# Attention over a cache with a gated FFN, one decode step: rounds of two heads on halves of the partitions, for single heads on all of them

## The chip, the cores and the metric

The kernel runs on one core of a Trainium2 chip. A core has TensorE (PE in the profile; PEld is its weight load), VectorE (DVE), ScalarE (ACT), GpSimd (POOL) and SyncE (SP), which here only issues transfers; sixteen DMA engines carry what SP and ACT issue. The metric is the device time of one execution in microseconds (us), the median of several runs; lower is better. A profile is one further execution, taken by the hardware profiler; its span is a little shorter than its time.

## The reference

```python
# B = 2, D = 448, H = 16 heads, Sk = 4096, Dh = 256, F = 1792, all float32
q = (x @ wq).reshape(B, 1, H, Dh).transpose(0, 2, 1, 3)
scores = einsum("bhqd,bhkd->bhqk", q, k_cache) * Dh ** -0.5
p = softmax(scores)
a = einsum("bhqk,bhkd->bhqd", p, v_cache).transpose(0, 2, 1, 3).reshape(B, 1, H * Dh) @ wo
h = maximum(x @ w1 + b1, 0) ** 2
b = h @ w2 + b2
g = sigmoid((x * gate_w).sum(-1))
out = g * a + (1 - g) * b
```

K and V are 2 x 16 x 4096 x 256 float32, 134 MB each; wq and wo are 7.3 MB each, w1 and w2 3.2 MB each. There is one query per batch row, so every byte of K and V is used once.

## The kernel before

The kernel goes through 32 pairs (batch b, head h), `pairs`, with b changing fastest. For a pair the 4096 keys lie as 32 consecutive keys on each of 128 partitions: one load of 4 MB (`load_kv`, line 131), a row of 32 KB for each partition, contiguous in memory. VectorE multiplies K by q in place (`times_q`, line 289, in pieces of 4, 12 and 16 keys, `LEAD` and `LEAD2`) and sums the rows (`row_sums`, line 296) into 32 scores a partition. `maximum` (line 302) takes the largest over a partition on VectorE and over the partitions with a matmul against the identity; `softmax` (line 309) has ScalarE write the exponentials into `pw`, a tensor in which every pair has its own two columns. `values` (line 335) multiplies V by these weights in 16 matmuls (two records each in the profile), four of which stand side by side in the array, and collects in one of two PSUM tiles, `po_bufs`. A unit is a group of heads that collect in one tile: four heads each, and at the end three and one. When a unit is done, `norm` works out the normalising factors, `take` copies the tile out, `turn` transposes it and normalises it, and `project` multiplies it by that unit's part of wo (8 matmuls) into `acc`. The last unit's part of wo and most of w2 go instead through `late` into `fin` at the very end.

All of K, V, wq, w1, w2 and wo come through one ring of five slots of 32 KB a partition (`ring`). A load into a slot can be issued only when everything has been read that the slot held before. Almost all loads are issued by SP in the order of the code, so an issue that waits for its slot holds back all issues behind it; loads already issued go on. In pair i the code issues K of pair i+1, then V of pair i, and then wq, w1, w2 or wo where one is due (w1 at i = 2, 0.46 MB of w2 at i = 4, wo of a unit at its last pair). The code is in the engines' order (`manual_schedule`): nothing reorders it. VectorE works one pair ahead of PE: in pair i it takes the maximum of pair i, then multiplies and sums K of pair i+1.

wq (448 x 4096) comes in three loads of 256, 128 and 64 input rows; the last 64 rows are laid on 128 partitions in two halves. `project_q` does 32 matmuls, four for each load and column block, and `make_q` spreads q of two heads at a time over the partitions.

Of the kernel before, what the change touches and what calls it, by code (L numbers as in the profile page):

```python
# [8 lines left out]
F32 = mybir.dt.float32  # L9
# [7 lines left out]
def kernel(  # L17
# [14 lines left out]
    nc = tc.nc  # L32
# [5 lines left out]
    CF = D // P  # L38
    R0 = CF * P
    RR = D - R0  # L40
    assert 2 * RR == P and B == 2 and CF == 3
    NK = S // P
    J = 32
    NCH = NK // J
# [7 lines left out]
    QH = QB // DH  # L52
    DQ = D // 4
    RING = 5
    WH = 2
    W2_CUTS = (4, 8, 11)
    LEAD = 4
# [4 lines left out]
    ring = ctx.enter_context(tc.tile_pool(name="ring", bufs=RING))  # L62
# [8 lines left out]


    wq_t = []

    def load_wq():

        ta = slot("wqa")
        nc.sync.dma_start(ta, wq[:2 * P, :].rearrange("(p c) n -> p (c n)", c=2))
        tb_ = slot("wqb")
        nc.sync.dma_start(tb_[:, :N], wq[2 * P:R0, :])  # L80
        nc.sync.dma_start(tb_[:, N:N + N // 2], wq[R0:, :].rearrange("r (s n) -> (r s) n", s=2))  # L81
        wq_t.extend([ta[:, :N], ta[:, N:], tb_[:, :N], tb_[:, N:N + N // 2]])

    w1_t = []

    def load_w1():
        t = slot("w1")
        nc.sync.dma_start(t[:, :2 * F], w1[:2 * P, :].rearrange("(p c) n -> p (c n)", c=2))
        nc.sync.dma_start(t[:, 2 * F:3 * F], w1[2 * P:R0, :])
        nc.sync.dma_start(t[:, 3 * F:3 * F + F // 2], w1[R0:, :].rearrange("r (s n) -> (r s) n", s=2))  # L90
        w1_t.extend([t[:, :F], t[:, F:2 * F], t[:, 2 * F:3 * F], t[:, 3 * F:3 * F + F // 2]])
# [39 lines left out]
    def load_kv(src, i, nm, cuts=(), between=None):  # L131
        b, h = pairs[i]
        v = src[b, h].rearrange("(n p j) d -> n p j d", p=P, j=J)
        tiles = []
        for n in range(NCH):
            t = slot(f"{nm}{b}_{h}_{n}").rearrange("p (j d) -> p j d", d=DH)
            at = [0, *(cuts if n == NCH - 1 else ()), J]
            for lo, hi in zip(at, at[1:]):
                nc.sync.dma_start(t[:, lo:hi, :], v[n, :, lo:hi, :])
                if between is not None and hi < J:  # L140
                    between()
            tiles.append(t)
        return tiles

    pairs = [(b, h) for h in range(H) for b in range(B)]
    last = len(pairs) - 1


    load_wq()
# [25 lines left out]
    for k in range(HG):  # L175
        for b in range(B):
            pw[k, b] = const.tile([P, NK // 2, 4 * HG], F32, name=f"pw{k}_{b}")
            nc.vector.memset(pw[k, b], 0.0)

# [6 lines left out]
    xr2 = const.tile([B, RR, 2], F32, name="xr2")  # L186
    nc.vector.tensor_copy(xr2, x2[:, R0:].unsqueeze(2).to_broadcast([B, RR, 2]))
    pxt = ps.tile([P, 512], F32, name="pxt", tag="sm")
    pxv = pxt[:, :(CF + 1) * B].rearrange("p (c b) -> p c b", b=B)
    for c in range(CF + 1):  # L190
        src = (x2[:, c:2 * P:2] if c < 2 else x2[:, c * P:(c + 1) * P] if c < CF
               else xr2.rearrange("b r s -> b (r s)"))
        nc.tensor.matmul(pxv[:, c, :], src, ident[:B, :B], start=True, stop=True)
    xT = const.tile([P, CF + 2, B], F32, name="xT")
    nc.vector.tensor_copy(xT[:, :CF, :], pxv[:, :CF, :])
    for s in range(2):
        nc.vector.tensor_scalar(xT[:, CF + s, :], pxv[:, CF, :], eo[:, s:s + 1], None, op0=ALU.mult)
# [19 lines left out]
    qs = const.tile([P, NQ // 4, QB], F32, name="qs")  # L217

    def project_q():
        for c in range(CF + 1):  # L220
            for n in range(NQ):
                a, gq = divmod(n, 4)
                if c < CF:
                    lt, rhs = xT[:, c, :], wq_t[c][:, n * QB:(n + 1) * QB]
                else:
                    half, m = divmod(n, NQ // 2)
                    lt, rhs = xT[:, CF + half, :], wq_t[c][:, m * QB:(m + 1) * QB]
                nc.tensor.matmul(po_bufs[a][32 * gq:32 * gq + B, :], lt, rhs, start=(c == 0), stop=(c == CF))  # L228
        for a in range(NQ // 4):
            nc.scalar.activation(qs[:, a, :], po_bufs[a], AF.Copy, scale=scale)  # L230
# [3 lines left out]
    def make_q(b, n):  # L234

        a, gq = divmod(n, 4)
        r = 32 * gq + b
        pq = ps.tile([P, 512], F32, name=f"pq{b}_{n}", tag="pq")
        nc.tensor.matmul(pq, ident[:, r:r + 1].to_broadcast([P, P]), qs[:, a, :], start=True, stop=True)  # L239
        t = work.tile([P, QB], F32, name=f"q{b}_{n}", tag=f"q{b}")  # L240
        nc.scalar.activation(t, pq, AF.Copy)  # L241
        for k in range(QH):
            q_sb[b, n * QH + k] = t[:, k * DH:(k + 1) * DH]
# [6 lines left out]
    h_sb = shared[:B, :F]  # L250

    def ffn_hidden():
        ph = ps.tile([P, 512], F32, name="ph", tag="pq")
        for c in range(CF + 1):
            for n in range(FB):
                if c < CF:
                    lt, rhs = xT[:, c, :], w1_t[c][:, n * D:(n + 1) * D]
                else:
                    half, m = divmod(n, FB // 2)
                    lt, rhs = xT[:, CF + half, :], w1_t[c][:, m * D:(m + 1) * D]  # L260
                nc.tensor.matmul(ph[32 * n:32 * n + B, :D], lt, rhs, start=(c == 0), stop=(c == CF))
        for n in range(FB):
            nc.scalar.activation(h_sb[:, n * D:(n + 1) * D], ph[32 * n:32 * n + B, :D], AF.Copy)

    def ffn_turn():
        hv = h_sb.rearrange("b (p c) -> b c p", c=FC)
        pt = ps.tile([P, FC, B], F32, name="pt", tag="sm")
        for c in range(FC):
            nc.tensor.matmul(pt[:, c, :], hv[:, c, :], ident[:B, :B], start=True, stop=True)  # L269
        return pt  # L270

    def ffn_square(pt):
        hb = const.tile([P, FC, B], F32, name="hb")
        nc.vector.tensor_tensor(hb, pt, b1T.unsqueeze(2).to_broadcast([P, FC, B]), op=ALU.add)
# [5 lines left out]
    kts, s_t, rs_t, rl_t, oT = {}, {}, {}, {}, {}  # L280

    def parts(lo, hi):

        while lo < hi:
            e = min(hi, (lo // J + 1) * J)
            yield lo // J, lo % J, lo % J + e - lo
            lo = e

    def times_q(i, lo, hi):

        b, h = pairs[i]
        for n, a, e in parts(lo, hi):
            kt = kts[i][n][:, a:e, :]
            nc.vector.tensor_tensor(kt, kt, q_sb[b, h].unsqueeze(1).to_broadcast([P, e - a, DH]), op=ALU.mult)  # L294

    def row_sums(i, lo, hi):
        if lo == 0:
            s_t[i] = work.tile([P, NK], F32, name=f"s{i}", tag="s")
        for n, a, e in parts(lo, hi):
            nc.vector.tensor_reduce(s_t[i][:, n * J + a:n * J + e], kts[i][n][:, a:e, :], axis=AX.X, op=ALU.add)  # L300

    def maximum(i):
# [3 lines left out]
        nc.tensor.matmul(mt[:, :P], m.to_broadcast([P, P]), ident, start=True, stop=True)  # L306
        return mt

    def softmax(i, mt):
        b, h = pairs[i]  # L310
        nb = work.tile([P, 1], F32, name=f"nb{i}", tag="nb")
        nc.vector.tensor_reduce(nb, mt[:, :P], axis=AX.X, op=ALU.max, negate=True)  # L312
        u, k = unit_of[h]
        c = B * k + b
        if c == 0:
            rs_t[u] = work.tile([P, B * len(units[u])], F32, name=f"rs{u}", tag="rs")
        nc.scalar.activation(pw[k, b][:, :, 2 * c:2 * c + 2], s_t[i].rearrange("p (m s) -> p m s", s=2), AF.Exp,  # L317
                             bias=nb, accum_out=rs_t[u][:, c:c + 1])

    def sums(u):  # L320
        sm = ps.tile([P, 512], F32, name=f"sum{u}", tag="sm")
        nc.tensor.matmul(sm[:, :B * len(units[u])], ones_pp, rs_t[u], start=True, stop=True)  # L322
# [12 lines left out]
    def values(i, vt, lo=0, hi=NK // 2):  # L335
        b, h = pairs[i]
        u, k = unit_of[h]
        n = len(units[u])
        po = po_bufs[u % 2]
        for m in range(lo, hi):  # L340
            r = 32 * (m % 4)
            j = 2 * m
            nc.tensor.matmul(po[r:r + 4 * n, :], pw[k, b][:, m, :4 * n],  # L343
                             vt[j // J][:, j % J:j % J + 2, :].rearrange("p j d -> p (j d)"),
                             start=(k == 0 and b == 0 and m < 4), stop=(k == n - 1 and b == B - 1 and m >= NK // 2 - 4))
# [56 lines left out]
    kts[0] = load_kv(k_cache, 0, "k")  # L402
    project_q()
    make_q(0, 0)
    make_q(1, 0)
    for n in range(NCH):
        times_q(0, n * J, (n + 1) * J)
# [123 lines left out]
```

## Time and profile before

| | us |
|---|---|
| median of 3 runs (lowest to highest) | 683.41 (683.37 to 683.63) |
| the profiled execution | 683.23 |
| its span | 681.4 |
| PE busy | 296.5 (44%) |
| VectorE busy | 581.1 (85%) |
| ScalarE busy | 37.9 (6%) |

An engine that is busy for a large share of the span need not be what the time hangs on. In this profile three things are to be read together: the row of the DMA engines' busy share, the rate in GB/s in a stretch that is clear of the start and the end, and what SP waited for before it issued. The two stretches in which the transfers are not at full rate, the first and the last slice, are the start and the end of the program.

### The profile page before, as it was taken

To read this page: it belongs to the slowest core of one execution; us is meant where nothing else is said; L and a number is where in the kernel's file an instruction comes from. 1 tells how busy PE (TensorE), PEld (TensorE's weight loads), DVE (VectorE), ACT (ScalarE), POOL (GpSimd) and SP (SyncE) were. 2 spreads that over 40 slices of the span, in tenths; PEclk is the share of its full clock that TensorE was granted. 3 is DMA by queue.
4 is the path that set the end of the run, shared out by engine and by line. 5 is a ranking of instruction groups with operands and counts; after the bars stand their busy time and mean duration, and the time that the engine had idled before them with its cause. 6 is when DMAs were issued, how large, how long until landed. Compare 5 with 4: busy or idle time off the path is not lost.

```text
span 681.4 us, 3865 instructions
## 1 busy us (share of the span) xinstructions
PE 296.5 (44%) x1598; PEld 96.8 (14%) x1598; DVE 581.1 (85%) x233; ACT 37.9 (6%) x113; POOL 0.7 (0%) x6
## 2 busy tenths in 40 slices
PE   4413445543359134433347543422455712443066
PEld 1000111400115001000014110000112200101013
DVE  3299997989896999999996999899997899999990
ACT  0200001000010000000001000000001000000000
POOL 0000000000000000000000000000000000000000
PEclk9856667787656776665667865567667757667579
DMA  8999999999999999999999999999999999999996
GB/s 370 435 433 435 430 425 431 426 434 436 431 437 430 431 431 431 430 431 431 432 426 441 431 431 432 433 429 431 431 430 423 432 431 431 430 435 437 423 419 270
DMA packets 12380, 289.79 MB, mean 425 GB/s; under 512 B 1478, under 2 KB 1612, under 8 KB 2892
## 3 DMA queue, kind: packets, MB, share of 16 engines
q1 hardware_dynamic: 12200, 289.55, 99.1%
q8 instruction: 12, 0.20, 0.1%
q10 hardware_dynamic: 164, 0.02, 0.0%
q14 instruction: 4, 0.03, 0.0%
HBM read 289.56 MB, written 0.00 MB: 425 GB/s over the span
## 4 chain that ended last, share of the span: by engine, by line
DMA 59%; DVE 37%; PE 2%; issue 0%; SPq 0%; ACT 0%; DVEq 0%; ACTq 0%
DMA k<-in_A_k_cache_dram 56%; DVE k L294 18%; DVE s L300 18%; DMA w<-in_B_w_dram 3%; PE acc L385 1%; PE po_buf L343 1%; DVE nb L312 0%; PE mt L306 0%; DVE m L304 0%; PE fin L390 0%; SPq L111 0%; ACT oT L378 0%; SPq L81 0%; ACT pw L317 0%; SPq L80 0%
## 5 line engine op out<-in xcount | busy, mean ns | idle before, releaser
L294 DVE TENSOR_TENSOR k<-k,q 128x3072 f32<-128x3072 f32 (+3 forms) x94 | 285.1, 3057 | 75.7 <-DMA k<-in_A_k_cache_dram 75.7
L300 DVE TENSOR_REDUCE s<-k 128x32 f32<-128x8192 f32 x32 | 278.0, 8686 | 2.2
L343 PE MATMUL po_buf<-v,pw 128*16 128x512 f32 (+2 forms) x1024 | 181.1, 857 | 218.3 <-DMA v<-in_A_v_cache_dram 217.4
L343 PEld LDWEIGHTS po_buf<-v,pw 128*16 128x16 f32 (+2 forms) x1024 | 36.7, 123 | 349.8 <-issue 319.7
L306 PE MATMUL mt<-ident,m 128*128 128x128 f32 x64 | 19.1, 389 | 136.2 <-DVE m L304 136.2
L317 ACT ACTIVATE pw<-s,nb 128x32 f32<-128x32 f32 x32 | 10.3, 323 | 544.0 <-DVE nb L312 544.0
L306 PEld LDWEIGHTS mt<-ident,m 128*128 128x128 f32 x64 | 11.9, 233 | 167.7 <-DVE m L304 117.1
L385 PE MATMUL acc<-wo,oT 128*2 128x448 f32 x48 | 22.9, 640 | 4.9 <-ACT oT L378 4.9
L239 PE MATMUL pq<-qs,ident 128*128 128x512 f32 x32 | 24.6, 868 | 0.0
L372 PEld LDWEIGHTS ot<-rl,shared 128*128 128x128 f32 x96 | 18.8, 304 | 0.0
L372 PE MATMUL ot<-rl,shared 128*128 128x8 f32 x96 | 18.8, 338 | 0.0
L312 DVE TENSOR_REDUCE nb<-mt 128x1 f32<-128x128 f32 x32 | 9.1, 284 | 1.7 <-PE mt L306 1.7
L241 ACT ACTIVATE q<-pq 128x512 f32<-128x512 f32 x16 | 9.4, 588 | 9.5 <-PE pq L239 9.5
L322 PE MATMUL sum<-rs,ones_pp 128*128 128x8 f32 (+2 forms) x10 | 2.8, 349 | 11.3 <-ACT pw L317 11.3
L354 ACT ACTIVATE shared<-po_buf 128x1024 f32<-128x1024 f32 x6 | 5.8, 1020 | 30.9 <-PE po_buf L343 30.9
L385 PEld LDWEIGHTS acc<-wo,oT 128*2 128x2 f32 x48 | 4.3, 94 | 21.3 <-issue 16.2
L239 PEld LDWEIGHTS pq<-qs,ident 128*128 128x128 f32 x32 | 6.9, 262 | 1.3 <-ACT qs L230 0.9
L269 PE MATMUL pt<-ident,shared 2*128 2x2 f32 x28 | 7.0, 378 | 0.0
L269 PEld LDWEIGHTS pt<-ident,shared 2*128 2x128 f32 x28 | 6.9, 336 | 0.1
L304 DVE TENSOR_REDUCE m<-s 128x1 f32<-128x32 f32 x32 | 5.9, 186 | 1.1
L317 ACT ACTIVATION_READ_ACCUMULATOR pw<-s,nb 128x1 f32 x32 | 6.0, 187 | 0.0
L228 PE MATMUL po_buf<-wqa,xT 128*2 128x512 f32 x32 | 5.6, 858 | 0.8 <-DMA wqa<-in_A_wq_dram 0.8
(62 smaller groups left out, 55.3 us busy)
## 6 DMA issues: line engine op xcount, KB each, us to landing
k<-in_A_k_cache_dram SPq DMA_DIRECT2D x32, 4096.0 KB, 40.0
v<-in_A_v_cache_dram SPq DMA_DIRECT2D x30, 4096.0 KB, 31.6
wo<-in_A_wo_dram SPq DMA_DIRECT2D x4, 1792.0 KB, 34.1
v<-in_A_v_cache_dram SPq DMA_DIRECT2D x3, 2048.0 KB, 25.9
wqa<-in_A_wq_dram SPq DMA_DIRECT2D x1, 4096.0 KB, 12.4
w<-in_B_w_dram SPq DMA_DIRECT2D x3, 896.0 KB
wqb<-in_A_wq_dram SPq DMA_DIRECT2D x1, 2048.0 KB, 16.9
v<-in_A_v_cache_dram SPq DMA_DIRECT2D x2, 1024.0 KB, 24.5
```

What stands on the lines that cost most here:

```text
L239: nc.tensor.matmul(pq, ident[:, r:r + 1].to_broadcast([P, P]), qs[:, a, :], start=True, stop=True)
L241: nc.scalar.activation(t, pq, AF.Copy)
L269: nc.tensor.matmul(pt[:, c, :], hv[:, c, :], ident[:B, :B], start=True, stop=True)
L294: nc.vector.tensor_tensor(kt, kt, q_sb[b, h].unsqueeze(1).to_broadcast([P, e - a, DH]), op=ALU.mult)
L300: nc.vector.tensor_reduce(s_t[i][:, n * J + a:n * J + e], kts[i][n][:, a:e, :], axis=AX.X, op=ALU.add)
L304: nc.vector.tensor_reduce(m, s_t[i], axis=AX.X, op=ALU.max)
L306: nc.tensor.matmul(mt[:, :P], m.to_broadcast([P, P]), ident, start=True, stop=True)
L312: nc.vector.tensor_reduce(nb, mt[:, :P], axis=AX.X, op=ALU.max, negate=True)
L317: nc.scalar.activation(pw[k, b][:, :, 2 * c:2 * c + 2], s_t[i].rearrange("p (m s) -> p m s", s=2), AF.Exp, bias=nb, accum_out=rs_t[u][:, c ...
L343: nc.tensor.matmul(po[r:r + 4 * n, :], pw[k, b][:, m, :4 * n], vt[j // J][:, j % J:j % J + 2, :].rearrange("p j d -> p (j d)"), start=(k = ...
L372: nc.tensor.matmul(ptv[:, j, :], ov[:, s, j, :], rl_t[u][:, :, s], start=(s == 0), stop=(s == 1))
L385: nc.tensor.matmul(acc[:, :D], oT[g][:, j, :], wo_sb[g][:, j, :], start=False, stop=(g == NG - 2 and j == HJ - 1))
```

## The change

A round is now two heads of one batch row: head 2n on partitions 0 to 63 and head 2n+1 on partitions 64 to 127, each partition with 64 consecutive keys. There are 16 rounds. K of a round is loaded in two halves of 32 keys a partition (`load_k`, line 138 of the changed kernel), each 4 MB in rows of 32 KB that lie 64 KB apart in memory; V in two such loads as well, but into one tile (`load_v`). The five slots become a ring of three slots of 32 KB, for K, w1, w2 and wo, and one slot of 64 KB (`wide`), for wq and then V. SP's order in round i is V of round i, then w1, w2 or wo where due (w1 at round 1, w2 at round 3, wo of a unit at the unit's last round), then the second half of K of round i+1 and the first half of K of round i+2. `units` ends with two units of two heads. A unit is taken, turned and projected in the round in which it ends, not in the next. wq and w1 come in one load each: seven half rows of the input matrix stand on a partition, and `times_x` adds them up in seven steps with four rows of x instead of two, 28 and 14 matmuls.

```diff
-    RING = 5
+    V_CUTS = (32, 48, 56)
-    ring = ctx.enter_context(tc.tile_pool(name="ring", bufs=RING))
+    ring = ctx.enter_context(tc.tile_pool(name="ring", bufs=3))
+    wide = ctx.enter_context(tc.tile_pool(name="wide", bufs=1))
...
+    def wide_slot(name):
+        return wide.tile([P, NK * DH], F32, name=name, tag="wide")
...
     def load_wq():
+        t = wide_slot("wq")[:, :D * N // P]
+        nc.sync.dma_start(t, wq.rearrange("(r k) (s n) -> (r k s) n", k=XR, s=2).rearrange(
+            "(p k) n -> p (k n)", k=XR))
+        return t
...
+    rounds = [(b, n) for n in range(H // 2) for b in range(B)]
+    last = len(rounds) - 1
+
+    def of_round(src, i):
+        b, n = rounds[i]
+        return src[b, 2 * n:2 * n + 2].rearrange("h (p j) d -> (h p) j d", p=PH)
+    def load_k(i, half):
+        t = slot(f"k{i}_{half}").rearrange("p (j d) -> p j d", d=DH)
+        nc.sync.dma_start(t, of_round(k_cache, i)[:, half * J:(half + 1) * J, :])
+        kts[i, half] = t
+    def load_v(i, cuts=(J,)):
+        t = wide_slot(f"v{i}").rearrange("p (j d) -> p j d", d=DH)
+        at = [0, *cuts, NK]
+        for lo, hi in zip(at, at[1:]):
+            nc.sync.dma_start(t[:, lo:hi, :], of_round(v_cache, i)[:, lo:hi, :])
+        return t
...
-    units = [list(range(g * HG, (g + 1) * HG)) for g in range(NG - 1)] + [list(range(H - HG, H - 1)), [H - 1]]
+    units = [list(range(g * HG, (g + 1) * HG)) for g in range(NG - 1)] + [[H - 4, H - 3], [H - 2, H - 1]]
...
+    def times_x(out, t, width, n):
+        for a in range(XR):
+            c, half = divmod(a, 2)
+            for g in range(n):
+                nc.tensor.matmul(out[32 * g:32 * g + 2 * B, :width], xT[:, half, c].rearrange("p s b -> p (s b)"),
+                                 t[:, (a * n + g) * width:(a * n + g + 1) * width],
+                                 start=(a == 0), stop=(a == XR - 1))
...
+        for e in range(2):
+            at = slice(e * PH, (e + 1) * PH)
+            c = B * (k + e) + b
+            nc.scalar.activation(pw[k, b][at, :, 2 * c:2 * c + 2], s_t[i][at].rearrange("p (m s) -> p m s", s=2), AF.Exp,
+                                 bias=nb[at], accum_out=rs_t[u % 2][at, c:c + 1])
...
+    load_k(0, 0)
+    load_k(0, 1)
+    load_k(1, 0)
     project_q()
+    make_q(0)
+    make_q(1)
...
+    for i, (b, n) in enumerate(rounds):
+        u, k = unit_of[2 * n]
+        done = b == B - 1 and k == len(units[u]) - 2
+        vt = load_v(i, V_CUTS) if i == last else load_v(i)
+        if i == 1:
+            w1_t = load_w1()
+        if i == 3:
+            load_w2_early()
+        if done and u < NG - 1:
+            load_wo(u)
         if i == last - 1:
+            load_wo(NG - 1)
         if i == last:
             load_w2_late()
         if i < last - 1:
+            load_k(i + 1, 1)
+            load_k(i + 2, 0)
+        if i == last - 2:
+            load_k(last, 1)
+        mt = maximum(i)
         if i < last:
+            times_q(i + 1, 0, 0, LEAD)
         softmax(i, mt)
...
+        values(i, vt)
+        if done:
+            take(u)
+            turn(u)
+            if u < NG - 1:
+                project(u)
...
+        rest(i + 1)
...
+    values(last, vt, p2, p3)
     late_wo(H - 3)
+    values(last, vt, p3, NK // 2)
     take(NG)
-    late_wo(H - 2)
     turn(NG)
     late_w2(0, W2_CUTS[0])
+    late_wo(H - 2)
     late_wo(H - 1)
```

SP's queue where the first unit (heads 0 to 3) ends, before. A name has the batch row and the head (`v1_3` is V of batch row 1, head 3), `wo0` is the unit's part of wo.

```order
L139 DMA v0_3_0_447<-in_A_v_cache_dram 128x8192
L139 DMA k0_4_0_481<-in_A_k_cache_dram 128x8192
L139 DMA v1_3_0_483<-in_A_v_cache_dram 128x8192
L125 DMA wo0_485<-in_A_wo_dram 128x3584
L139 DMA k1_4_0_528<-in_A_k_cache_dram 128x8192
L139 DMA v0_4_0_530<-in_A_v_cache_dram 128x8192
```

The same place now. A name has the round, and K its half (`k4_1` is the second half of K of round 4).

```order
L102 DMA w2_0_420<-in_B_w2_dram 128x896
L122 DMA wo0_422<-in_A_wo_dram 128x3584
L141 DMA k4_1_424<-in_A_k_cache_dram 128x8192
L141 DMA k5_0_426<-in_A_k_cache_dram 128x8192
L148 DMA v4_522<-in_A_v_cache_dram 128x8192 x2
L141 DMA k5_1_525<-in_A_k_cache_dram 128x8192
```

The small part of w2 now stands next to wo, both in the ring of three, behind V of round 3 and ahead of both halves of K.

PE's queue at the end of the first unit, before: values of the last two heads, with maxima (`mt`) and the sums between, turn (L372) and projection (L385).

```order
L343 MATMUL po_buf0_92<-v0_3_0_447,pw3_0_111 16x512 x16
L306 MATMUL mt7_489<-ident_85,m7_487 128x128
L322 MATMUL sum0_496<-rs0_206,ones_pp_90 128x8
L239 MATMUL pq1_2_503<-qs_145,ident_85 128x512
L343 MATMUL po_buf0_92<-v1_3_0_483,pw3_1_113 16x512 x16
L306 MATMUL mt8_534<-ident_85,m8_532 128x128
L372 MATMUL ot0_542<-rl0_501,shared_147 128x8 x16
L385 MATMUL acc_96<-wo0_485,oT0_559 2x448 x8
```

And now:

```order
L308 MATMUL mt3_430<-ident_85,m3_428 64x64 x2
L325 MATMUL sum0_439<-rs0_107,ones_pp_90 128x8
L345 MATMUL po_buf0_92<-v3_417,pw2_1_105 16x512 x32
L373 MATMUL ot0_480<-rl0_444,shared_145 128x8 x16
L386 MATMUL acc_96<-wo0_422,oT0_497 2x448 x8
L464 MATMUL acc_96<-w2_0_420,hT_144 2x448 x2
```

The values of a round are 32 matmuls in a row, and turn and projection follow them with no maximum between.

SP's queue at the end of the program, before:

```order
L139 DMA k0_15_0_1361<-in_A_k_cache_dram 128x8192
L139 DMA k1_15_0_1363<-in_A_k_cache_dram 128x8192
L139 DMA v1_14_0_1365<-in_A_v_cache_dram 128x8192
L139 DMA v0_15_0_1408<-in_A_v_cache_dram 128x4096
L128 DMA wo3_1410<-in_A_wo_dram 128x4x896
L139 DMA v0_15_0_1408<-in_A_v_cache_dram 128x4096
L139 DMA v1_15_0_1449<-in_A_v_cache_dram 128x4096
L139 DMA v1_15_0_1449<-in_A_v_cache_dram 128x2048 x2
```

And now:

```order
L141 DMA k15_1_1157<-in_A_k_cache_dram 128x8192
L148 DMA v14_1228<-in_A_v_cache_dram 128x8192 x2
L125 DMA wo3_1231<-in_A_wo_dram 128x4x896
L148 DMA v15_1281<-in_A_v_cache_dram 128x8192
L148 DMA v15_1281<-in_A_v_cache_dram 128x4096
L148 DMA v15_1281<-in_A_v_cache_dram 128x2048 x2
```

Of the last loads only wo stands between V of the last two rounds, which share a slot.

More of the change, by code (lines that the diff above doesn't have):

```diff
@@ L37 @@
     N = H * DH
[L38 to L44, printed above, removed]
+    XR = 7
+    XC = (XR + 1) // 2
+    assert D * 2 == P * XR and B == 2
+    PH = P // 2
+    NK = S // PH
+    J = NK // 2
     HG = 4
@@ L129, in load_wo @@
             wo_sb[g] = tv.rearrange("p (h j n) -> p h j n", h=HG, j=NJ)
[L131 to L149, printed above, removed]
+    rounds = [(b, n) for n in range(H // 2) for b in range(B)]
[3 more added lines that the diff above has]
+        return src[b, 2 * n:2 * n + 2].rearrange("h (p j) d -> (h p) j d", p=PH)
+    kts = {}
+    def load_k(i, half):
[7 more added lines that the diff above has]
+            nc.sync.dma_start(t[:, lo:hi, :], of_round(v_cache, i)[:, lo:hi, :])
+        return t
+    wq_t = load_wq()
     x2 = const.tile([B, D], F32, name="x2")
@@ L178 @@
             nc.vector.memset(pw[k, b], 0.0)
+    rs_t = []
+    for n in range(2):
+        rs = const.tile([P, B * HG], F32, name=f"rs{n}")
+        nc.vector.memset(rs, 0.0)
+        rs_t.append(rs)
     eo = const.tile([P, 2], F32, name="eo")
@@ L214 @@
     nc.tensor.matmul(acc[:, :D], gd[:, 1, :], b2r, start=True, stop=False)
-    qs = const.tile([P, NQ // 4, QB], F32, name="qs")
+    qs = const.tile([P, QB], F32, name="qs")
     def project_q():
[L220 to L230, printed above, removed]
@@ L232 @@
-    q_sb = {}
[L234 to L243, printed above, removed]
+        times_x(po_bufs[0], wq_t, QB, NQ // 2)
@@ new lines, in project_q, with make_q @@
+        nc.scalar.activation(qs, po_bufs[0], AF.Copy, scale=scale)
+    q_sb = {}
+    def make_q(i):
+        b, n = rounds[i]
+        a, g = divmod(n, NQ // 2)
+        r = 32 * g + B * a + b
+        pq = ps.tile([P, 512], F32, name=f"pq{i}", tag="pq")
+        for k in range(2):
+            nc.tensor.matmul(pq[k * PH:(k + 1) * PH, :DH], ident[:, r:r + 1].to_broadcast([P, PH]),
+                             qs[:, k * DH:(k + 1) * DH], start=True, stop=True)
+        q_sb[i] = work.tile([P, DH], F32, name=f"q{i}", tag=f"q{b}")
+        nc.scalar.activation(q_sb[i], pq[:, :DH], AF.Copy)
@@ L246, with ffn_hidden @@
     hT = const.tile([P, FC, B], F32, name="hT")
     shared = const.tile([P, 2 * HG * DH], F32, name="shared")
-    h_sb = shared[:B, :F]
-    def ffn_hidden():
+    h_sb = shared[:2 * B, :F]
+    def ffn_hidden(w1_t):
         ph = ps.tile([P, 512], F32, name="ph", tag="pq")
[L254 to L263, printed above, removed]
+        times_x(ph, w1_t, D, FB // 2)
+        hv = h_sb.rearrange("r (a g n) -> r g a n", a=2, n=D)
+        for g in range(FB // 2):
+            nc.scalar.activation(hv[:, g], ph[32 * g:32 * g + 2 * B, :D].unsqueeze(1).to_broadcast([2 * B, 2, D]), AF.Copy)
@@ L273, in ffn_square @@
         hb = const.tile([P, FC, B], F32, name="hb")
-        nc.vector.tensor_tensor(hb, pt, b1T.unsqueeze(2).to_broadcast([P, FC, B]), op=ALU.add)
+        for a in range(2):
+            at = slice(a * PH, (a + 1) * PH)
+            nc.vector.tensor_tensor(hb[at], pt[at, :, a * B:(a + 1) * B], b1T[at].unsqueeze(2).to_broadcast([PH, FC, B]),
+                                    op=ALU.add)
         nc.vector.tensor_scalar(hb, hb, 0.0, None, op0=ALU.max)
@@ L335, in values @@
     def values(i, vt, lo=0, hi=NK // 2):
-        b, h = pairs[i]
-        u, k = unit_of[h]
+        b, h = rounds[i]
+        u, k = unit_of[2 * h]
         n = len(units[u])
@@ L341, in values @@
             r = 32 * (m % 4)
[L342 to L345, printed above, removed]
+            nc.tensor.matmul(po[r:r + 4 * n, :], pw[k, b][:, m, :4 * n], vt[:, 2 * m:2 * m + 2, :].rearrange("p j d -> p (j d)"),
+                             start=(k == 0 and b == 0 and m < 4), stop=(k == n - 2 and b == B - 1 and m >= NK // 2 - 4))
     o_sb = {}
@@ L444 @@
         if done:
             norm(u, sums(u))
-        if h % QH == QH - 1 and h + 1 < H:
-            make_q(b, (h + 1) // QH)
-        if k == 0 and b == 0 and u > 0:
-            turn(u - 1)
-            if u < NG:
-                project(u - 1)
+        if i == last:
+            break
+        values(i, vt)
[4 more added lines that the diff above has]
+                project(u)
+        if i == 1:
+            ffn_hidden(w1_t)
+        if i == 2:
+            pt = ffn_turn()
@@ L471 @@
-        if i < last - 1:
-            values(i, vt)
-            if done:
-                take(u)
-        if i == last - 1:
-            rest(last)
-            values(i, vt, 0, NK // 4)
-            values(i, vt, NK // 4, 3 * NK // 8 + 2)
-            mt = maximum(last)
-            values(i, vt, 3 * NK // 8 + 2)
-        elif i < last - 2:
-            rest(i + 1)
-        if i == 4:
+        rest(i + 1)
+        if i == 2:
             ffn_square(pt)
-    q4 = NK // 8
-    values(last, vt, 0, 2 * q4)
@@ L489 @@
-    values(last, vt, 2 * q4, 3 * q4)
+    p1, p2, p3 = (c // 2 for c in V_CUTS)
+    values(last, vt, 0, p1)
+    values(last, vt, p1, p2)
     late_wo(H - 4)
+    values(last, vt, p2, p3)
     late_wo(H - 3)
-    values(last, vt, 3 * q4, 4 * q4)
+    values(last, vt, p3, NK // 2)
     take(NG)
-    late_wo(H - 2)
     turn(NG)
     late_w2(0, W2_CUTS[0])
+    late_wo(H - 2)
     late_wo(H - 1)
```

134 lines of the change are left out of this document (43 added, 91 removed).

## The prediction

> **What bounds the kernel now.** I read the page first: the two DMA rows over 40 slices and the total that was read.
>
> ```profile
> DMA  8999999999999999999999999999999999999996
> GB/s 370 435 433 435 430 425 431 426 434 436 431 437 430 431 431 431 430 431 431 432 426 441 431 431 432 433 429 431 431 430 423 432 431 431 430 435 437 423 419 270
> HBM read 289.56 MB, written 0.00 MB: 425 GB/s over the span
> ```
>
> The sixteen DMA engines are full from the first slice to the last but one. The windows say when they start and at what rate they run (columns: stretch, length, busy of PE, its loads, DVE, ACT, POOL, clock granted to PE, DMA share, GB/s).
>
> ```profile
> 0.00:30.00 30.00, 15.30 (x80) 4.68 (x80) 5.83 (x24) 5.16 (x7) 0.70 (x6) 0.96 0.96 403
> 300.00:600.00 300.00, 129.26 (x630) 40.91 (x626) 268.05 (x97) 16.01 (x51) 0.00 (x0) 0.65 1.00 431
> 676.00:681.40 5.40, 1.58 (x60) 0.96 (x48) 0.00 (x0) 0.26 (x1) 0.00 (x0) 1.00 0.06 21
> ```
>
> At 431 GB/s the 289.56 MB take 671.8 us of the 681.4 us span: **the transfers are the bound**, and what is left is a start of 2 us and an end of 7 us. A 4 MB load (4.194 MB) costs 9.73 us. The chain of waits ends as transfers do, and its first and last rows give two latencies that I need.
>
> ```profile
> 0.74 0.39 SPq L78
> 2.19 28.04 DMA k<-in_A_k_cache_dram
> 30.33 8.70 DVE k L294
> ...
> 653.98 23.29 DMA w<-in_B_w_dram
> 677.27 0.04 issue
> 677.32 0.99 PE fin L390 x32
> ```
>
> 403 GB/s over 30 us is 12.09 MB, 28.05 us of work at full rate, so data flowed from 1.95: **1.2 us from issue to flow** on an empty queue (issue at 0.74). wq and the first K are 11.53 MB, through at 28.7; VectorE saw them at 30.23: **1.5 us from last byte to landing**. The waits of SP's queue show why nothing starves today:
>
> ```profile
> SPq L139 <- DVE m L304: 485.2, 29, 25.1
> SPq L139 <- PE acc L385: 45.7, 3, 15.8
> ```
>
> SP, not the DMA engines, does the waiting, for ring slots, and there is always a load or two queued below it. So one question decides the change: **is there a place where SP is held until the queued loads have run out?** Each us of that is a us of the total.
>
> **The change part by part.** Prices of the consumers, from the groups and from the stretch in which a unit of four heads closes (columns: start, length, engine and line, operation, count):
>
> ```profile
> L300 DVE TENSOR_REDUCE s<-k 128x32 f32<-128x8192 f32 x32 | 278.0, 8686 | 2.2
> L294 DVE TENSOR_TENSOR k<-k,q 128x8192 f32<-128x8192 f32 x1 | 8.7, 8693 | 20.1 <-DMA k<-in_A_k_cache_dram 20.1
> L304 DVE TENSOR_REDUCE m<-s 128x1 f32<-128x32 f32 x32 | 5.9, 186 | 1.1
> L317 ACT ACTIVATE pw<-s,nb 128x32 f32<-128x32 f32 x32 | 10.3, 323 | 544.0 <-DVE nb L312 544.0
> 136.16 5.51 PE L343 MATMUL po_buf<-v,pw 128*16 128x512 f32 x32 [3.81 <-DMA v<-in_A_v_cache_dram]
> 219.73 3.60 PE L343 MATMUL po_buf<-v,pw 128*16 128x512 f32 x29
> 598.48 6.44 PE L343 MATMUL po_buf<-v,pw 128*12 128x512 f32 x32 [8.66 <-DMA v<-in_A_v_cache_dram]
> 202.24 1.94 ACT L354 ACTIVATE shared<-po_buf 128x1024 f32<-128x1024 f32 x2 [11.19 <-PE po_buf L343]
> 204.79 6.77 PE L372 MATMUL ot<-rl,shared 128*128 128x8 f32 x32
> 524.66 5.88 PE L372 MATMUL ot<-rl,shared 128*128 128x8 f32 x32
> 211.60 0.73 ACT L378 ACTIVATE oT<-ot 32x16 f32<-32x16 f32 x4
> 212.39 7.12 PE L385 MATMUL acc<-wo,oT 128*2 128x448 f32 x15 [0.82 <-ACT oT L378]
> ```
>
> Bytes, VectorE's elements and the values' matmuls stay as they are; a round is two old steps. A round takes 4 x 9.73 = 38.9 us of DMA and, on VectorE, 4 x 8.69 us and about 1 us of small operations: 35.8 us, so VectorE goes on waiting about 3 us a round for the second half of K.
>
> *Small operations.* Half as many maxima (0.19 us each), matmuls of 64 columns for 128 in the maximum, four fewer memsets, two exponentials a round on half the partitions with twice the elements (0.32 us each at 32 elements), two q copies of half the width. ACT and PE have idle time in every round for these, VectorE its 3 us: cost 0, and without that cover well under 0.5 us a round.
>
> *V in one 64 KB slot.* The next V is issued when the values of this one are done. From the last byte of V: 1.5 landing, 5.5 for the second half's 32 matmul records, 1.2 to flow: 8.2 us, while two K halves (19.5 us) are queued. Covered, with 11 us over, in every round but the last, where there is no K left.
>
> *Head.* wq is usable only when all 7.34 MB are there: 1.95 + 17.0 + 1.5 = 20.5 instead of 13.16.
>
> ```profile
> 13.16 5.56 PE L228 MATMUL po_buf<-wqa,xT 128*2 128x512 f32 x32 [0.80 <-DMA wqa<-in_A_wq_dram]
> 18.54 3.93 PE L228 MATMUL po_buf<-wqb,xT 128*2 128x512 f32 x32
> ```
>
> The 56 records that replace these 64 take 5.56 + 24/32 x 3.93 = 8.5 us, so q is projected at 29 and, with two activations and a small matmul, VectorE starts at about 31.5, 1.2 us later than today. V(0) needs the wq slot (29), while three K halves keep the queue busy until 48.2. Later in the ramp V(1) has 7 us of cover; the tightest is K(3,0): it waits for the row sums of round 2's first half at about 120, flows at 121.3, and the queue (V(1), w1, K(2,1)) lasts until 123.7. Cost 0; were q 4 us later, 2 us.
>
> *Round 3, the first loss.* The loads stand as K(3,1), K(4,0), V(3) twice, w2's first 0.46 MB, wo of unit 0 (1.84 MB), K(4,1), K(5,0), V(4). w2 and wo take two of the three ring slots, so **K(4,1) goes into the slot of K(4,0)**, which VectorE must finish first, and **K(5,0) into that of wo**, which is free after the unit's projection. Count from the last byte of K(3,1), for which VectorE is waiting. Landing 1.5; second half of round 3, 2 x 8.69; FFN square and maximum 1.2 (six operations like the 0.19 us one); first half of round 4, 17.7 (2 x 8.69 and a small reduction between); normalising 0.5 (three more): K(4,0) is free at 38.3, its successor flows at 39.5. The queue before it holds 3 x 9.73 + 1.06 + 4.26 = 34.5. **5.0 us idle.** K(4,1) then runs until 49.2. Meanwhile V(3) has its last byte at 29.2: 1.5 landing, 5.5 values, 2.1 take, 6.3 turn, 0.8 copies, 7.5 projection (7.12 for 15 of its 16 records) and 0.2 between engines make 53.1; K(5,0) flows at 54.3. **5.1 us idle.** While SP is held, V(4) and K(5,1) are queued behind it, and PE and VectorE wait for these. The sum, 10.1, hangs on the second chain alone, 54.3 - 34.5 - 9.7; a faster VectorE would only move idle time from the first place to the second. Bounds: with values as at 219.73 (4.0) and turn as at 524.66, 8; if PE stays at half clock in the projection (as in the 6.44 us row), its 16 records go from 7.5 to 12 us and the values to 6.8: 16. Nothing absorbs this, as all else is slack of other engines.
>
> In rounds 7 and 11 only wo enters the ring. K(9,0) waits for half of round 8: by the same count it may flow at 38.5, and the queue holds 43.2. Covered by 4 to 5 us.
>
> *The end, the second loss.* V(15) needs the whole slot of V(14), and behind V(14) only the last wo is queued; w2's rest stands behind V(15). From V(14)'s last byte: 1.5 + 5.5 + 0.1 + 1.2 = 8.3 us; the last wo is 1.84 MB at the rate of the window below, 4.7 us. **3.6 us idle** (2 to 5 by the same two rows of the values). Today V(31) sits in a slot of its own and waits for no such thing.
>
> ```profile
> 649.50:653.50 4.00, 3.56 (x24) 0.59 (x16) 4.00 (x2) 0.36 (x1) 0.00 (x0) 0.69 0.98 389
> 654.00:664.00 10.00, 5.29 (x36) 1.51 (x35) 9.86 (x3) 0.22 (x2) 0.00 (x0) 0.74 1.01 427
> ```
>
> *Tail.* After the last V piece PE has 8 records of values, take, turn, 32 records of wo and 96 of w2, while w2's rest lands about 6 us later:
>
> ```profile
> 671.32 1.04 PE L343 MATMUL po_buf<-v,pw 128*4 128x512 f32 x8 [0.68 <-DMA v<-in_A_v_cache_dram]
> 673.08 1.10 PE L372 MATMUL ot<-rl,o 128*128 128x2 f32 x8 [0.34 <-ACT o L358]
> 674.12 0.95 PE L390 MATMUL fin<-w,hT 128*2 128x112 f32 x32
> ```
>
> 1.0 + 0.8 + 1.1 + 1.0 + 1.0 + 1.0 = 6: the last 32 still wait for the last landing, as now. Two more columns in turn(NG) and 16 records moved behind it cost 0; without that cover, 0.6 us.
>
> *Rows.* Today's last two V are cut into more pieces (about 8 MB, the 427 window against 431: 0.2 us), and wq and w1 become one load each: -0.3 us, between 0 and -0.6. Rows of K and V stay 32 KB, now at every 64 KB. The trace has no such load; nearest are the last V pieces, 16 KB at every 32 KB, in the 427 window, which a plain shorter row would explain as well. I take 0; with 427 for all 268.4 MB of K and V it is +5.8 us.
>
> Sum against the profiled run, 683.23 us (span 681.4 and 1.8 around it, 0.2 below the median of 683.41): 683.2 + 10.1 + 3.6 - 0.3 = **696.6 us**.
>
> **The rivals.** *PE slow in the two chains*: 683.2 + 16 + 5 - 0.3 = 704. For it: the clock row of 0.65 in the middle; against it: turn and projection repeat within 1 us in the closings shown.
>
> *Strided halves read slower*, by something in the memory: 702 by the 427 window. Against it: that window is within 1% of full rate although its rows are strided. The Trainium skill (DMA: Bandwidth & Descriptors, Latency and other measured facts) has copies of 16 KB rows that lose rate at row pitches of large powers of two, 207 GB/s at 512 KB against 214; an estimate from that, 3.3% of K and V's 623 us, would give 717. No run here shows such a pitch.
>
> *Only the end's wait is real*, because K(4,1) or wo is freed earlier than I count: 683.2 + 3.6 = 687.
>
> *Not slower*: strided halves read faster. At the moment each load is one contiguous 4 MB; from two heads at a time the engines may find memory less in each other's way. It decides from 441 GB/s on K and V (268.4 MB in 608.6 instead of 622.8 us, 14 us less), which gives 683 or below. One slice of 40 shows 441, the mean of 300 us is 431, so the row speaks against it. By the Trainium skill (DMA: Bandwidth & Descriptors, Where 436 GB/s comes from) the ports end at 435 GB/s, which the 431 here agrees with; by that rule no more than 6 us could come back.
>
> **How the numbers follow.** Forecast 0.76 (its own range 692 to 701), PE slow 0.09, strided slower 0.07, end alone 0.04, not slower 0.04 (half of it within 0.2%, which is about what a measurement can tell from no change). So slower 0.96, same 0.02, faster 0.02. The range of 691.5 to 705 leaves out the last two and the upper part of the strided rival.
>
> **What would show it.** Right: two slices of low GB/s at about 200 to 220 us and one near 660 us, no others between; SP issuing K(4,1) at the end of a row sum, K(5,0) at the end of the projection, V(15) at the end of the values; the rate elsewhere 431; VectorE and PE no busier. Wrong: full DMA slices at 200 us (the slots come free earlier), a rate other than 431 in the middle rounds (the pitch matters), or a gap at rounds 1, 7 or 11 (a cover of mine that is too thin).

## The result, and the profile after

| | us |
|---|---|
| before, median of 4 runs (lowest to highest) | 683.43 (683.37 to 683.63) |
| after, median of 4 runs | 695.65 (695.51 to 696.42) |
| ratio, 95% interval | 1.0181 (1.0163 to 1.0198) |
| span of the profiled execution, before and after | 681.4 and 694.6 |

The kernel is 12.2 us slower. The profiled execution of the changed kernel is the slowest of its four, 696.42 us, so that the spans differ by 13.2. One of the four executions of the kernel with the last V in the ring, below, was in a slow state that no other shared (745.65 us) and is left out of its time. The same rows of the page as before, of the changed kernel:

```profile
PE 261.0 (38%) x1618; PEld 83.1 (12%) x1618; DVE 571.8 (82%) x171; ACT 35.5 (5%) x110; POOL 0.7 (0%) x6
DMA  9999999999978999999999999999999999999896
GB/s 394 422 425 447 426 423 437 436 428 423 439 294 340 424 447 426 423 430 437 430 420 440 423 442 430 425 440 429 428 434 426 436 434 428 426 440 431 362 378 266
HBM read 289.56 MB, written 0.00 MB: 417 GB/s over the span
```

A slice is 17.4 us. Two neighbours at 191 to 226 us and two at 643 to 677 us are short of data; every other slice between the first and the last is at 420 GB/s or more. PE and VectorE do less work than before, and the time went up. So the loss has two places. The windows (columns as in the prediction) put a size on them, and show that the rate elsewhere has not moved:

```profile
190.00:207.00 17.00, 12.71 (x82) 6.63 (x75) 11.64 (x2) 2.64 (x6) 0.00 (x0) 0.80 0.71 287
207.00:225.00 18.00, 10.02 (x23) 1.94 (x21) 11.20 (x2) 0.38 (x1) 0.00 (x0) 0.78 0.82 340
652.00:670.00 18.00, 5.80 (x36) 1.34 (x36) 17.10 (x4) 0.07 (x1) 0.00 (x0) 0.79 0.81 326
300.00:600.00 300.00, 112.78 (x630) 34.35 (x634) 265.82 (x72) 15.38 (x52) 0.00 (x0) 0.66 1.00 431
```

What a window lacks of 431 GB/s, in time: 17 x (1 - 287/431) = 5.7 us, 18 x (1 - 340/431) = 3.8 us and 18 x (1 - 326/431) = 4.4 us, together 13.9. That is the 13.2 us of the spans to within 1 us, which is about what windows of this length can say, since packets lie across their edges. The DMA share in the same rows gives less: 17 x (1 - 0.71), 18 x (1 - 0.82) and 18 x (1 - 0.81) are 4.9, 3.2 and 3.4 us, together 11.6. The two ways of counting lie on either side of the 13.2, so each gap has a size to about 1 us.

Who held SP is read from the timeline around the two places (columns: start, length, engine, line, operation, count, and in brackets the idle time before it and who ended it; merged rows cover several instructions, and SP's length then runs to the end of the last).

```profile
192.99 8.69 DVE L300 TENSOR_REDUCE s<-k 128x32 f32<-128x8192 f32 x1
194.14 3.63 PE L345 MATMUL po_buf<-v,pw 128*16 128x512 f32 x32 [1.74 <-DMA v<-in_A_v_cache_dram]
197.90 1.94 ACT L355 ACTIVATE shared<-po_buf 128x1024 f32<-128x1024 f32 x2 [12.13 <-PE po_buf L345]
199.89 5.09 PE L373 MATMUL ot<-rl,shared 128*128 128x8 f32 x30 [0.53 <-ACT shared L355]
201.71 13.58 SPq L141 DMA_DIRECT2D k<-in_A_k_cache_dram  x2
205.81 9.13 PE L386 MATMUL acc<-wo,oT 128*2 128x448 f32 x16 [0.82 <-ACT oT L379]
213.77 8.69 DVE L295 TENSOR_TENSOR k<-k,q 128x8192 f32<-128x8192 f32 x1 [12.09 <-DMA k<-in_A_k_cache_dram]
215.40 0.85 SPq L148 DMA_DIRECT2D v<-in_A_v_cache_dram  x2
...
655.03 5.32 PE L345 MATMUL po_buf<-v,pw 128*8 128x512 f32 x32 [4.42 <-DMA v<-in_A_v_cache_dram]
660.41 1.86 SPq L148 DMA_DIRECT2D v<-in_A_v_cache_dram  x4
```

SP issues K(4,1) at 201.71, when VectorE has ended the row sums of K(4,0) (192.99 + 8.69). The second K of that row is K(5,0): its issue ends at 201.71 + 13.58 = 215.29, so it began when the projection ended (205.81 + 9.13 = 214.94). V(15) is issued at 660.41, when the values of round 14 end (655.03 + 5.32). VectorE, which never stands for more than 8.4 us at a time between 225 and 640 us, stands for 12.09 us before K(4,1).

### The profile page after: what moved, and what is told of

The parts are those of the page before. It is cut to its first block, busy times and chain, and to the rows that moved or that the text cites. A ratio compares the mean times of both kernels' runs of the same rounds, so it can differ in the third digit from the quotient of the medians.

```text
span 694.6 us, 3778 instructions
## 1 busy us (share of the span) xinstructions
PE 261.0 (38%) x1618; PEld 83.1 (12%) x1618; DVE 571.8 (82%) x171; ACT 35.5 (5%) x110; POOL 0.7 (0%) x6
## 2 busy tenths in 40 slices
DMA packets 11660, 289.79 MB, mean 417 GB/s; under 512 B 1398, under 2 KB 1532, under 8 KB 2556
## 3 DMA queue, kind: packets, MB, share of 16 engines
q1 hardware_dynamic: 11480, 289.54, 97.4%
## 4 chain that ended last, share of the span: by engine, by line
DMA 64%; DVE 23%; PE 11%; SPq 1%; ACT 1%; issue 1%; ACTq 0%
DMA v<-in_A_v_cache_dram 49%; DMA k<-in_A_k_cache_dram 12%; DVE k L295 11%; DVE s L300 11%; PE po_buf L345 6%; DMA wq<-in_A_wq_dram 3%; PE acc L386 1%; PE po_buf L215 1%; PE ot L373 1%; SPq L148 1%; PE fin L391 1%; ACT shared L355 0%; SPq L141 0%; ACT o L359 0%; ACT oT L379 0%
## 5 line engine op out<-in xcount | busy, mean ns | idle before, releaser
L295 DVE TENSOR_TENSOR k<-k,q 128x4096 f32<-128x4096 f32 (+3 forms) x63 | 281.6, 4486 | 90.5 <-DMA k<-in_A_k_cache_dram 72.0
L345 PE MATMUL po_buf<-v,pw 128*16 128x512 f32 (+1 forms) x1024 | 163.4, 796 | 81.3 <-DMA v<-in_A_v_cache_dram 66.3
L308 PE MATMUL mt<-ident,m 128*64 128x64 f32 x64 | 7.7, 335 | 309.7 <-DVE m L304 309.7
L345 PEld LDWEIGHTS po_buf<-v,pw 128*16 128x16 f32 (+1 forms) x1024 | 31.7, 116 | 198.5 <-issue 116.4
L319 ACT ACTIVATE pw<-s,nb 64x64 f32<-64x64 f32 x32 | 11.2, 349 | 344.7 <-DVE nb L314 344.3
L252 PE MATMUL pq<-qs,ident 128*64 128x256 f32 x64 | 10.7, 419 | 0.7 <-ACT qs L241 0.7
L215 PE MATMUL po_buf<-wq,xT 128*4 128x512 f32 x56 | 7.9, 729 | 4.8 <-DMA wq<-in_A_wq_dram 4.8
L215 PE MATMUL ph<-w,xT 128*4 128x448 f32 x28 | 7.0, 661 | 3.9 <-DMA w<-in_B_w_dram 3.9
L386 PEld LDWEIGHTS acc<-wo,oT 128*2 128x2 f32 x48 | 4.6, 100 | 20.8 <-issue 18.0
L276 PEld LDWEIGHTS pt<-ident,shared 4*128 4x128 f32 x28 | 6.9, 336 | 0.9 <-issue 0.9
L276 PE MATMUL pt<-ident,shared 4*128 4x4 f32 x28 | 7.0, 380 | 0.0
L252 PEld LDWEIGHTS pq<-qs,ident 128*64 128x64 f32 x64 | 3.3, 138 | 11.9 <-issue 10.1
```

The source lines that it names most:

```text
L215: nc.tensor.matmul(out[32 * g:32 * g + 2 * B, :width], xT[:, half, c].rearrange("p s b -> p (s b)"), t[:, (a * n + g) * width:(a * n + g + ...
L252: nc.tensor.matmul(pq[k * PH:(k + 1) * PH, :DH], ident[:, r:r + 1].to_broadcast([P, PH]), qs[:, k * DH:(k + 1) * DH], start=True, stop=True)
L276: nc.tensor.matmul(pt[:, c, :], hv[:, c, :], ident[:2 * B, :2 * B], start=True, stop=True)
L295: nc.vector.tensor_tensor(kt, kt, q_sb[i].unsqueeze(1).to_broadcast([P, hi - lo, DH]), op=ALU.mult)
L308: nc.tensor.matmul(mt[at, :PH], m.to_broadcast([P, PH]), ident[:, at], start=True, stop=True)
L319: nc.scalar.activation(pw[k, b][at, :, 2 * c:2 * c + 2], s_t[i][at].rearrange("p (m s) -> p m s", s=2), AF.Exp, bias=nb[at], accum_out=rs_ ...
```

## The experiments

### One ring slot instead of two in round 3

```diff
         if g < NG - 1:
+            if g == 0:
+                t2 = t[:, HJ * D:(HJ + WH) * D].rearrange("p (c n) -> p c n", n=D)
+                for c in range(WH):
+                    w2_sb[c] = t2[:, c, :]
+                nc.sync.dma_start(t2, w2_v[:, :WH, :])
             nc.sync.dma_start(tv, wo_g[g])
...
-        if i == 3:
-            load_w2_early()
```

> The small part of w2 shares the ring slot of the first unit's wo, so that one slot and not two is taken from K in round 3. Theory (the loss is SP held for ring slots in round 3 and for the V slot at the end): both gaps of round 3 go, 4.9 and 3.0 us and the two restarts, and the end's gap stays: 687 us (686 to 688.5). SP issues K(5,0) at the end of a row sum about 3 us before the queue is empty. Rival (the second gap belongs to the projection chain whatever slot K(5,0) has, as PE is late for V): 5 us come back, 690.5 us. Rival (strided rows cost the time): 695.6 us, unchanged.

Measured: 688.06 us (686.22 to 688.9), 1.0058 of the kernel before (1.0041 to 1.0075). 7.6 us came back. Windows of the two places, of this kernel:

```profile
190.00:230.00 40.00, 22.43 (x116) 8.82 (x112) 32.36 (x8) 3.90 (x11) 0.00 (x0) 0.76 1.00 427
640.00:665.00 25.00, 10.71 (x62) 2.37 (x54) 21.61 (x8) 0.88 (x4) 0.00 (x0) 0.64 0.77 314
```

In round 3 the rate is 427 where the changed kernel has 332 over the same 40 us: both gaps are gone, although PE goes through the same values, turn and projection there. That takes away the rival in which the second gap belongs to PE's chain as such; the chain mattered because K(5,0) had to have the slot at its end. Now K(5,0) hangs on a row sum: its issue ends at 182.61 + 19.64 = 202.25, just after VectorE's row sums of K(4,0) have ended in that profile, at 201.90.

```profile
182.61 19.64 SPq L146 DMA_DIRECT2D k<-in_A_k_cache_dram  x2
```

The gap at the end is still there, and in the profiled execution (688.9 us, the slowest) it is larger than the 4.4 us of the changed kernel: 25 x (1 - 314/431) = 6.8 us. There PE took 6.27 us for the same 32 records that took 5.32 above, which is 1 us of the 2.4; no cause is shown for the rest. The row is from that profile:

```profile
647.04 6.27 PE L350 MATMUL po_buf<-v,pw 128*8 128x512 f32 x32 [3.67 <-DMA v<-in_A_v_cache_dram]
```

### The first half of the last V in the ring

```diff
+    def load_v_last(i, cuts):
+        ta = slot(f"v{i}a").rearrange("p (j d) -> p j d", d=DH)
+        nc.sync.dma_start(ta, of_round(v_cache, i)[:, :J, :])
+        tb = wide_slot(f"v{i}").rearrange("p (j d) -> p j d", d=DH)
+        at = [*cuts, NK]
+        for lo, hi in zip(at, at[1:]):
+            nc.sync.dma_start(tb[:, lo:hi, :], of_round(v_cache, i)[:, lo:hi, :])
+        return ta, tb
...
+            v = vt if i < last else vt[2 * m // J]
...
-        vt = load_v(i, V_CUTS) if i == last else load_v(i)
+        vt = load_v_last(i, V_CUTS) if i == last else load_v(i)
```

> The first half of the last V goes into a ring slot, the second half into the upper half of the wide slot. Theory: the end's gap of 3.5 us and its restart go, the two of round 3 stay: 691.7 us (690.5 to 692.5). Rival (the end is bound by PE's tail after the last V piece, so that an earlier V is not worth its gap): 694 us or more. Rival (strided rows): 695.6 us.

Measured, in three runs: 692.52 us (691.13 to 692.66), 1.0126 of the kernel before (1.0109 to 1.0143), 3.1 us less than the changed kernel and at the upper edge of the range that was expected. The two low slices of round 3 stay (296 and 336 GB/s), the ones near the end are 414 and 427. SP's timeline of this kernel shows how: the first half of V is issued at the end of a row sum, 9 us ahead of the second half, which still waits for the values.

```profile
651.14 0.33 SPq L146 DMA_DIRECT2D v15a<-in_A_v_cache_dram  x1
660.11 1.28 SPq L150 DMA_DIRECT2D v<-in_A_v_cache_dram  x3
```

### Both edits

The two diffs above together.

> Both edits. Theory: the three gaps make up the difference to the kernel before but for the tail's 0.8 us: 683.3 us (682.5 to 684.5), within 0.2% of the kernel before, and no slice under 415 GB/s but the first and the last. Rival (each gap that goes opens another of its size, since VectorE has only 3 us a round to spare): 688 us or more. Rival (strided rows): 695.6 us.

Measured, in ten runs: 683.34 us (683.03 to 684.22), 1.0001 of the kernel before (0.9991 to 1.001). The page:

```profile
DMA  9999999999999999999999999999999999999996
GB/s 378 439 433 433 430 433 427 430 433 433 431 422 431 430 433 433 435 431 432 431 425 438 431 428 431 431 433 430 431 431 428 433 431 431 432 431 433 413 431 265
```

No gap is left and none has opened elsewhere. Rounds of two heads, a ring of three and one slot for V cost nothing where the queue is never let run dry; the 12.2 us were the three places, two in round 3 and one at the end. The two edits are not worth the same in either order. Singly they bring 7.6 and 3.1 us, together 10.7; both at once bring 12.3. Closing the end is worth 3.1 us while round 3 has its gaps and 4.7 us once they are gone (688.06 to 683.34). That goes with the larger gap at the end in the profile of the first edit, whose cause is in part open. One slice near the end is at 413, short of the 415 that I had set; it has the last wo, whose pieces of 3.5 KB moved at 389 GB/s before the change as well.

### The pitch alone

```diff
+    def whole(src, i, half):
+        b, n = rounds[i]
+        return src[b, 2 * n + half].rearrange("(p j) d -> p j d", p=P)
...
-        nc.sync.dma_start(t, of_round(k_cache, i)[:, half * J:(half + 1) * J, :])
+        nc.sync.dma_start(t, whole(k_cache, i, half))
...
-            nc.sync.dma_start(t[:, lo:hi, :], of_round(v_cache, i)[:, lo:hi, :])
+            nc.sync.dma_start(t[:, lo:hi, :], whole(v_cache, i, lo // J)[:, lo % J:lo % J + hi - lo, :])
```

> The changed kernel with every 4 MB load of K and V taken from one contiguous head, 32 KB a partition, instead of 32 KB at every 64 KB of two heads; slots, order and bytes as in the changed kernel, and its scores then mix the keys of two heads. Theory (waits for slots): unchanged, 695.6 us (695 to 696.5), 431 GB/s between 300 and 600 us as before. Rival (the pitch of 64 KB costs): faster by what it costs; 13 us if it were all of the loss. Rival (two heads at a time are read faster and hide part of the gaps' price): slower.

Measured: 696.98 us (694.39 to 698.84), 1.0195 of the kernel before (1.0169 to 1.0221), against 1.0181 (1.0163 to 1.0198) with the pitch. That is 0.5 us above the range that was expected. Between 300 and 600 us it moved 431 GB/s, as the changed kernel did.

```profile
300.00:600.00 300.00, 115.72 (x630) 36.20 (x634) 266.14 (x69) 15.38 (x52) 0.00 (x0) 0.65 1.00 431
```

So rows of 32 KB at every 64 KB, of two heads at a time, cost nothing that these runs can tell, and bring nothing; the times spread over 4.5 us, so they alone do not exclude a price of 1 or 2 us. The rate does exclude that the pitch is what costs 12 us: over the 623 us of K and V that would be 8 GB/s between the two kernels.

### PE's chain longer

```diff
                 project(u)
+            if u == 0:
+                spare = ps.tile([P, 512], F32, name="spare", tag="pq")
+                for j in range(HJ):
+                    nc.tensor.matmul(spare[:B, :D], oT[u][:, j, :], wo_sb[u][:, j, :], start=(j == 0), stop=(j == HJ - 1))
```

> After the first unit's projection its 8 matmuls are done once more, into a PSUM tile that nobody reads, so that wo's slot comes free later; the rest is the changed kernel. Theory (K(5,0) hangs on PE's chain to the end of the projection): the second gap grows from 3.0 us by 16 records of 0.375 us, 6 us (8 where PE runs at half clock), the first gap keeps its 4.9 us: 701.7 us (701 to 704). Rival (VectorE's chain sets the loss and PE's is hidden behind it): under 1 us more, 696.5 us.

Measured: 701.47 us (700.24 to 702.62), 5.8 us more than the changed kernel. PE's and SP's timelines of this kernel:

```profile
207.00 7.80 PE L386 MATMUL acc<-wo,oT 128*2 128x448 f32 x16 [0.82 <-ACT oT L379]
214.63 6.18 PE L461 MATMUL spare<-wo,oT 128*2 128x448 f32 x16
...
201.60 19.57 SPq L141 DMA_DIRECT2D k<-in_A_k_cache_dram  x2
```

6.18 us of matmuls whose result nobody reads cost 5.8 us of the whole: K(4,1) is issued as before, K(5,0) ends its issue at 221.17 instead of 215.29.

### VectorE's chain longer

```diff
         times_q(i, 0, LEAD2, J)
+        if i == 4:
+            spare = work.tile([P, 8], F32, name="spare", tag="spare")
+            nc.vector.tensor_reduce(spare, kts[i, 0][:, :8, :], axis=AX.X, op=ALU.add)
         row_sums(i, 0)
```

> One extra reduction of 2048 elements a partition (2.2 us) on VectorE ahead of the row sums that free the slot of K(4,0); nobody reads its result. Theory (the sum of the two gaps of round 3 hangs on PE's chain alone): the first gap grows by 2.2 us to 7.1, the second shrinks by as much to 0.8, the time stays at 695.7 us (695 to 697). Rival (VectorE's chain sets the loss): 2.2 us more, 697.9 us.

Measured: 696.51 us (695.62 to 696.63; the changed kernel 695.51 to 696.42). SP's timeline and two windows of this kernel:

```profile
203.71 11.64 SPq L141 DMA_DIRECT2D k<-in_A_k_cache_dram  x2
190.00:210.00 20.00, 15.65 (x86) 7.14 (x79) 13.68 (x3) 2.64 (x6) 0.00 (x0) 0.76 0.63 257
210.00:225.00 15.00, 7.08 (x19) 1.43 (x17) 9.11 (x2) 0.38 (x1) 0.00 (x0) 0.84 0.93 384
```

K(4,1) comes 2.0 us later, and K(5,0) ends its issue at 215.35, as in the changed kernel at 215.29. The first gap has grown to 20 x (1 - 257/431) = 8.1 us, the second has shrunk to 15 x (1 - 384/431) = 1.6; together 9.7 where it was 9.5, and the profiled spans of the two kernels are both 694.6. So in the profiled executions the two gaps of round 3 are one loss, set by PE's chain, and VectorE only decides where in it the idle time lies. The medians say it less sharply: this kernel's is 0.9 us higher, with three of its four runs above 696.4 where three of the changed kernel's are below 695.8. That is under half of the 2.2 us that the rival gives; what the 0.9 us are is open.

### V in one load

On top of both edits, V of rounds 0 to 13 comes in one load of 64 KB rows.

```diff
-        vt = load_v_last(i, V_CUTS) if i == last else load_v(i)
+        vt = load_v_last(i, V_CUTS) if i == last else load_v(i) if i == last - 1 else load_v(i, ())
```

> The kernel with both edits (e12_both), and V of rounds 0 to 13 in one load of 64 KB rows. In the profile of the changed kernel wq's 56 KB rows take 2.116 us in the median, 27.1 GB/s an engine, and 32 KB rows 1.215 us, 27.0. Theory (the transfers are the bound, and a row has a fixed price of some 13 ns): 8 rows fewer an engine and round, 14 rounds, 1.5 us: 681.8 us (681.3 to 682.8), below both kernels. Rival (values now start when the whole V is there, 11 us of PE instead of 5.5 after it, and V's slot comes too late): gaps, 684 us or more. Rival (rows are split into pieces of at most 32 KB anyway): 683.3 us, as e12_both.

Measured, in eleven runs: 682.39 us (681.97 to 682.93), 0.9984 of the kernel before (0.9976 to 0.9993): faster than both, by about 1 us. The DMA queue has 9464 packets instead of 11480, 2016 fewer: 14 rounds x 128 rows and 14 x 16 packets of under 512 B (1398 of these on the page with both edits, 1174 here), so a 64 KB row goes as one packet. These are the rows of that queue, first with both edits, then of this kernel:

```profile
q1 hardware_dynamic: 11480, 289.54, 99.1%
q1 hardware_dynamic: 9464, 289.54, 99.0%
```

The saving of 0.95 us against the kernel with both edits is less than the 1.5 I expected from 13 ns a row; it is the right size and sign, and not measured finely enough to say more.

## Why the prediction was right

**The bound.** That the transfers are the bound and a microsecond of empty queue is one of the time held: with the gaps closed the time is that of before to 0.1%, though PE and VectorE do less.

**The two latencies.** wq landed at 20.51 (20.5 was worked out), which bears out the two together and not each by itself. VectorE began at 30.27, not 31.5: the projection took 7.9 us and not 8.5, and the step from there to VectorE 1.8 and not 2.5. With the gaps closed nothing of the head is seen in the time. None of the covers that I counted as thin (K(3,0), K(9,0), K(13,0)) failed: no low slice there.

```profile
20.51 7.92 PE L215 MATMUL po_buf<-wq,xT 128*4 128x512 f32 x56 [4.85 <-DMA wq<-in_A_wq_dram]
```

**Round 3.** The mechanism and both slots are as predicted. The sum was put at 10.1 us; the windows show 9.5 by the rate and 8.2 by the DMA share. The first gap was put at 5.0 us and came to 5.7 or 4.9, the second at 5.1 and came to 3.8 or 3.2. The term that was too large is PE's chain from V's landing to the issue of K(5,0): I had 22.4 us, it took 20.8 (194.14 to 214.94). The second half of the values took 3.63 us for my 5.5, after PE had stood for only 1.74 us. The turn and its copies, from 199.84 to 205.81, took 6.0 for my 7.1. The projection took 9.13 for 7.5. These errors cancel in part, which is luck; with 20.8 in the place of 22.4 my own sum would have been 8.5. That the loss follows PE's chain is shown by the doubled projection, to 0.4 us; that VectorE's chain adds nothing is shown in the profile, and by the medians only to 0.9 us.

**The end.** 3.6 us predicted, 4.4 in the window by the rate and 3.4 by the DMA share, 3.1 by removing it alone and 4.7 by removing it after round 3; the chain of landing, values and issue is in the rows above.

**The tail.** I put it at 0, with 0.6 us if its cover failed. It failed in the profiled execution: after the last V piece the records of `late` took 1.67 us for 32, not 0.95, and the last 64 no longer waited for w2.

```profile
683.70 1.04 PE L345 MATMUL po_buf<-v,pw 128*8 128x512 f32 x8 [1.04 <-DMA v<-in_A_v_cache_dram]
686.67 1.67 PE L391 MATMUL fin<-w,hT 128*2 128x112 f32 x32
688.12 1.69 PE L391 MATMUL fin<-wo,oT 128*2 128x112 f32 x32
689.61 1.73 PE L391 MATMUL fin<-w,hT 128*2 128x112 f32 x64
```

In the kernel with both edits these come at 0.95 us for 32 and the last wait for w2 again:

```profile
674.18 0.95 PE L406 MATMUL fin<-w,hT 128*2 128x112 f32 x32
...
677.00 0.95 PE L406 MATMUL fin<-w,hT 128*2 128x112 f32 x32 [0.34 <-DMA w<-in_B_w_dram]
```

The 128 records go from 686.67 to 691.34 (689.61 + 1.73), 4.7 us, and there from 674.18 to 677.95, 3.8 us with the wait; that is some 0.9 us that belongs to the changed kernel's profiled execution and that my sum did not have. It is within the range. The clock granted to PE was 0.84 from 683 to 694 us here and 1.00 from 673 to 678 us with both edits; that a gap before it is what lowered the clock was not tried by itself.

**The rows.** No run shows the -0.3 us for fewer and larger pieces by itself. With the gaps closed, all the rest of the change together is worth -0.2 us (683.34 against 683.50), which is within what the runs can tell.

**The total.** 696.6 us were predicted on the basis of the profiled execution, and the profiled execution took 696.42. That is closer than the terms are: round 3 was put too high, by 0.6 to 1.9 us, and the tail, put at 0, took some 0.9.

**The rivals.** PE slow in both chains happened only in part (9.13 for the projection). Strided rows slower or faster: neither; the rate was 431 GB/s with and without the pitch. The loss that the Trainium skill has at pitches from 512 KB (DMA: Bandwidth & Descriptors, Latency and other measured facts) has no counterpart here at 64 KB. Only the end's wait real: no, closing it alone leaves 9 us.

## What to carry to other kernels

Where the transfers are the bound, as here, fewer and larger tiles are free only as long as something is queued behind every issue that waits for a slot: walk the issue queue in order, and at each wait compare the time to the release with the bytes already queued. Look first where the regular pattern is broken, here where two small weights take ring slots sized for 4 MB tiles, and where the stream ends. Where two waits follow each other, find the chain that ends last; in the profiles here a change of the other one only moved the gap.

## What the runs showed that was not expected

Some kernels in which PE's chain holds the queue vary more from run to run: 686.22 to 688.9, 694.39 to 698.84 and 700.24 to 702.62 us in four runs each, against 683.29 to 683.71 in thirteen runs of the kernel before. It is no rule: the four runs of the changed kernel lie within 0.9 us, and the ten with both edits, whose queue is full, within 1.2. PE took 3.63, 5.32 and 6.27 us for 32 records of values in the rows above (the first in round 3, the others in round 14), after 1.74, 4.42 and 3.67 us of standing idle. That such differences make the spread is not shown. With a full queue they do not reach the time: between 300 and 600 us PE was busy for 102.76 us with V in one load, 120.33 with both edits and 129.26 before, at 431 GB/s each time.
